# Attention with a two-pass gated layer behind it: the second pass's weights are decoded by other engines and at other points of the program

## The chip, the core and the metric

The kernel runs on one core of a Trainium2 chip. Its engines work side by side, each through its own list of instructions in order: PE (TensorE, matmuls, with its weight loads PEld), DVE (VectorE), ACT (ScalarE), POOL (GpSimd) and SP (SyncE), which here issues all DMAs. SBUF is the on-chip memory, PSUM holds the results of matmuls. The metric is the device time of one execution in microseconds.

## The reference

Eight batches of eight heads with 576 tokens of 64 features go through a linear attention with exponential features, and its output, as 4608 tokens of 512 features, through a gated layer of width 1536:

```python
def phi(x):
    proj = np.einsum('bhsd,df->bhsf', x, w_phi)
    proj = proj - np.max(np.abs(proj), axis=-1, keepdims=True)
    return np.concatenate([np.exp(proj), np.exp(-proj)], axis=-1)
q_p, k_p = (phi(q), phi(k))
kv = np.einsum('bhsf,bhsd->bhfd', k_p, v)
z = np.sum(k_p, axis=2)
num = np.einsum('bhsf,bhfd->bhsd', q_p, kv)
den = np.einsum('bhsf,bhf->bhs', q_p, z)[..., None] + 1e-06
x = (num / den).transpose(0, 2, 1, 3).reshape(4608, 512)
out = ((x @ w_a) * (x @ w_b)) @ w_out
```

The inputs `moe_w_a`, `moe_w_b` and `moe_w_out` reach the kernel in 64-bit floating point, as pairs of 32-bit words.

## The kernel before

**Precision.** Most matmuls are done on values split in two parts: `hi` is the value rounded to the matmul's format (fp32r), `lo` the rest, and a product is hi*hi + hi*lo + lo*hi. The helper `split` (L143 to L146) makes the parts: a cast on one engine (recorded as L139 on ACT), then a subtraction on another (recorded as L146).

**Stages.** The attention fills the first part. It writes unnormalised outputs to DRAM (`xun`) and the reciprocal denominators (`rec`). The gated layer runs in two passes over its width, slices of 128:

- *First pass*, six slices (`NFS[0]`), 16 blocks of 288 tokens, `moe_block(0, j)`. A block loads x (`load_x`: a DMA for x, DMAs for the reciprocals `rb`, the product L527, a split). Then for each slice f it makes `pa` and `pb` (12 matmuls each, L559), copies pa to SBUF on ACT (L563), multiplies on DVE (`h`, L564) and splits h into `hh` and `hl`. At the end, four outputs `po` of 18 matmuls each (L582), copied to `o` by ACT (L585) and written to the DRAM tensor `part`. So a block is 216 matmuls of 288 columns.
- *Second pass*, the other six slices, nine blocks of 512 tokens, `second_pass`. The slices are taken in three pairs q with Winograd's form of a 2x2 product (`winograd`, L642): it needs seven combinations of the weights for a and for b (`w11`, `w12`, `s1` to `s4`, `w22`) and the same of x (`factors_of_x`, L604 to L607). The results are gathered in `top` and `low` (L648 to L661), `h` is formed (L664 to L666) and split, and the outputs (`outputs`, L689) add `part` from DRAM (L694).

**The weights.** A raw load brings 128 x 512 pairs of words (`load_raw`, tile `raw`, two buffers). `decode` (L435 to L439) makes of them a rounded value s and a rest g with one ACT and four DVE instructions. `load_weights` makes `hi` and `lo` of a slice of w_out from them (L464 to L466). `load_factors` does it for a pair q and one of a and b: two decodes with a sum each (`w32`, L477), the sums s1 to s4 (L483 on DVE, L484 to L486 on POOL) and seven splits, with the cast on ACT and the subtraction on POOL. The places of the results (`places`) are 18 tiles of their own for the first pair and two `o` slices, and the places of the first pass's weights for the rest; those come free as the last block of the first pass uses them for the last time.

**Order.** The code is written as Python generators that yield between steps; the order in which they are drained is the program's order. The framework's scheduler then sets the order on each engine, with the program's order as its priority. While the attention runs, a queue `work` holds the blocks of the first pass whose x is ready, and they are drained at a pace between the attention's turns. Behind it, `ahead` (weights of pair 0 and two slices of w_out) and `more` (the remaining weights) are advanced a step at a time between the steps of the last blocks and of the second pass.

**PSUM.** The first pass's accumulators come from `ps_moe` with three buffers. `ps_late` with five buffers exists once the attention is over; a block takes the pool that was last appended to `pools_moe` when its first step runs (`psum = pools_moe[-1]`). Before the change that is `ps_moe` for blocks 0 to 13 and `ps_late` for 14 and 15.

Of the kernel before, what the change touches and what calls it, by code (L numbers as in the profile page):

```python
# [14 lines left out]
ALU = mybir.AluOpType  # L15
# [18 lines left out]
DECODE_TURN, X_LAG, BLOCK_LAG = 2, 2, 8  # L34
# [16 lines left out]

SLICES0 = 6
T2 = 512


@with_exitstack
def tile_kernel(ctx, tc, qT, km, kr, vm, vr, w_phi, w_a, w_b, w_out, out):
# [13 lines left out]
    nc = tc.nc  # L71
    B, H, _, S = qT.shape
# [7 lines left out]
    NCC = DM // P  # L80
    TS = (HALF, T2)
    NFS = (SLICES0, DF // P - SLICES0)
# [60 lines left out]
    def split(hi, lo, src, eng_hi, eng_lo):  # L143

        copy(eng_hi, hi, src)
        eng_lo.tensor_tensor(lo, src, hi, op=ALU.subtract)  # L146
# [274 lines left out]
    def decode(raw, u, stage):  # L421

        low, high = raw[:, :, 0], raw[:, :, 1]
        w = stage("w", [P, 2 * DM], F32, f"w_{u}")
        g, s = w[:, :DM], w[:, DM:]
        gb, sb = g.bitcast(U32), s.bitcast(U32)
        nc.scalar.mul(g, high.bitcast(F32), 2.0**-112)  # L435
        nc.vector.tensor_scalar(gb, gb, 3, None, op0=ALU.logical_shift_left)
        nc.vector.scalar_tensor_tensor(sb, high, 0x80000000, gb, op0=ALU.bitwise_and, op1=ALU.bitwise_or)
        nc.vector.tensor_scalar(gb, sb, 0xFF800000, None, op0=ALU.bitwise_and)
        nc.vector.scalar_tensor_tensor(g, low, 2.0**-52, g, op0=ALU.mult, op1=ALU.mult)  # L439
        return s, g  # L440

    def load_raw(p, f, nm, stage):

        cols = (sum(NFS[:p]) + f) * P
        src = {"a": w_a, "b": w_b, "o": w_out}[nm]
        raw = stage("raw", [P, DM, 2], U32, f"raw_{p}_{f}_{nm}")
        if nm == "o":
            nc.sync.dma_start(raw.rearrange("p n w -> p (n w)"), src[cols : cols + P, :].bitcast(U32))
        else:
            nc.sync.dma_start(  # L450
                raw.rearrange("p (c n) w -> p c (n w)", c=NCC),
                src.bitcast(U32)[:, 2 * cols : 2 * (cols + P)].rearrange("(c p) n -> p c n", p=P),
            )
        return raw

    def load_weights(p, f, names, stage, place=None):
        for nm in names:
            u = f"{p}_{f}_{nm}"
            s, g = decode(load_raw(p, f, nm, stage), u, stage)
            hi, lo = (  # L460
                pool.tile([P, DM], F32R, tag=tag, name=f"w{part}_{u}")
                for part, (pool, tag) in zip("hl", place or ((wpool, f"wh_{f}_{nm}"), (wpool, f"wl_{f}_{nm}")))
            )
            nc.scalar.copy(hi, s)  # L464
            nc.vector.tensor_tensor(s, s, hi, op=ALU.subtract)
            nc.vector.tensor_tensor(lo, s, g, op=ALU.add)  # L466
            weights[(p, f, nm)] = (hi, lo)
            yield

    def load_factors(q, nm, stage, places):  # L470

        w = []
        for i in range(2):
            u = f"q{q}_{nm}_{i}"
            s, g = decode(load_raw(1, 2 * q + i, nm, stage), u, stage)
            w.append(stage("w32", [P, DM], F32, f"w32_{u}"))
            nc.vector.tensor_tensor(w[i], s, g, op=ALU.add)  # L477
            yield
        n = DM // 2
        (w11, w12), (w21, w22) = ((t[:, :n], t[:, n:]) for t in w)  # L480
        sums = stage("ws", [P, 4, n], F32, f"ws_q{q}_{nm}")
        s1, s2, s3, s4 = (sums[:, i] for i in range(4))
        nc.vector.tensor_tensor(s1, w21, w22, op=ALU.add)  # L483
        nc.gpsimd.tensor_tensor(s3, w11, w21, op=ALU.subtract)  # L484
        nc.gpsimd.tensor_tensor(s2, s1, w11, op=ALU.subtract)
        nc.gpsimd.tensor_tensor(s4, w12, s2, op=ALU.subtract)  # L486
        factors = dict(w11=w11, w12=w12, s2=s2, s1=s1, s3=s3, w22=w22, s4=s4)
        yield
        for k, w32 in factors.items():
            pool, tag = places.popleft()  # L490
            t = pool.tile([P, 2, n], F32R, tag=tag, name=f"wf_q{q}_{nm}_{k}")
            split(t[:, 0], t[:, 1], w32, nc.scalar, nc.gpsimd)
            weights[(q, nm, k)] = t
            if k == "s1":
                yield
        yield

# [175 lines left out]
    def second_pass(xin):  # L673
        xs = yield from factors_of_x(0, xin)
        pool = xpools[1]
        for j in range(NT // T2):
# [38 lines left out]
            for cc in range(NCC):  # L715
                outputs(cc, range(0 if cc == NCC - 1 else early.stop, NFS[1]))
                yield

    def run(work, steps=None):

        while work and steps != 0:
            if next(work[0], work) is work:
                work.popleft()
            elif steps is not None:
                steps -= 1
# [3 lines left out]
    with ExitStack() as c:  # L729
        pools = attention_pools(c)  # L730
        consts = attention_consts(pools[0])
        work, tasks, due, st = deque(), {}, 0.0, {}
        tasks[DECODE_TURN] = []
        for names in ("ab", "o"):
            stage = stage_shared(pools[1])
            tasks[DECODE_TURN] += [load_weights(0, f, names, stage) for f in range(NFS[0])]
        for turn, ready in attention_steps(pools, consts, st):
            if ready is not None:
                at = turn + BLOCK_LAG
                tasks[at] = [moe_block(0, ready * per + h) for h in range(per)]  # L740
            for t in sorted(tasks):
                if t <= turn:
                    work.extend(tasks.pop(t))
            due += PACE0 if turn < PACE0_UNTIL else PACE
            run(work, int(due))
            due -= int(due)
        run(work)
    for t in sorted(tasks):
        work.extend(tasks[t])
    pools_moe.append(ctx.enter_context(tc.tile_pool(name="ps_late", bufs=5, space=PSUM)))  # L750


# [2 lines left out]
    ab = deque((wpool, f"w{part}_{f}_{nm}") for f in range(NFS[0]) for nm in "ab" for part in "hl")  # L755
# [7 lines left out]
    stage = stage_own(xin, 2, 2)  # L763
# [2 lines left out]
    )  # L766
    second = second_pass(xin)
    last = work.pop()
    while work:
        run(work, 1)  # L770
        next(ahead, None)
    next(last)
    for f in range(NFS[0]):
        next(last)
        next(ahead, None)
        if f < NCC // 2:
            next(second)
    for _ in ahead:
        pass
    more = itertools.chain(*(load_factors(1, nm, stage, ab) for nm in "ab"))  # L780
    for _ in range(NCC):
        next(more, None)
        next(last, None)
    run(deque([last]))
    xstack.close()
    xpools.append(ctx.enter_context(tc.tile_pool(name="pool", bufs=1)))
    ab.extend(o)
    more = itertools.chain(
        more,
        *(load_factors(2, nm, stage, ab) for nm in "ab"),  # L790
        *(load_weights(1, f, "o", stage, [o.pop(), o.pop()]) for f in range(2, NFS[1])),
    )
    for i, _ in enumerate(more):
        if i % 3 == 2:
            next(second)
    run(deque([second]))

# [32 lines left out]
```

## Time and profile before

| | us |
|---|---|
| median of three runs | 1281.06 |
| the three runs | 1281.87, 1281.06, 1276.15 |
| the profiled execution | 1278.22 |
| its span, first to last instruction | 1276.1 |
| block 11 begins on PE | 687.4 |
| block 15 begins on PE | 811.3 |
| second pass begins on PE | 843.2 |

In the lines of the profile, L is a line of the kernel, then come the engine, the operation and `out<-in`; a row of the timeline starts with its start and its duration in us, and ends with the idle time of the engine before it and who ended that. A table of stages gives the busy time and the count of instructions of each engine in a stretch of the span, then PE's granted clock (1.00 is full), the share of the DMA engines and GB/s.

### The profile page before, as it was taken

Reading aid. Unit: us, or ns where it says so; the run is one execution under the profiler, and the core shown is the slowest. Engines: PE = TensorE matmul, PEld = TensorE weight load, DVE = VectorE, ACT = ScalarE, POOL = GpSimd, SP = SyncE. Lnnn points to the kernel's source line nnn. Section 1 sums busy time; section 2 is a strip of 40 time slices with the busy share of each in tenths; the row PEclk is TensorE's granted clock in tenths of the full one; section 3 lists DMA queues with packets and bytes.
Section 4 is the critical chain, followed back from the end, with each engine's and each line's share of the span. In section 5 each row is a group of like instructions: output and inputs, shape, how many; then the busy total and the mean of one; then the engine's idle time right before and its main releaser. Section 6 shows DMA issues by size and latency. Waiting matters only on the chain.

```text
span 1276.1 us, 23003 instructions
## 1 busy us (share of the span) xinstructions
PE 1237.6 (97%) x8588; PEld 1136.0 (89%) x8588; DVE 935.3 (73%) x1622; ACT 734.4 (58%) x1577; POOL 214.5 (17%) x130
## 2 busy tenths in 40 slices
PE   8999999999999999999999899979999999999998
PEld 4566788999999999999999899979999999999997
DVE  7989568998999999988965873588656556556443
ACT  5667668889888988888873442444223223223221
POOL 2332222212122221312220500460000000000000
PEclk9999999999999999999999999989999999999999
DMA  7665443453534434444225451142422322331221
GB/s 185 177 196 151 116 122 88 112 141 78 145 96 133 115 104 125 110 113 121 71 57 152 145 162 57 46 129 88 127 82 74 116 91 66 108 93 57 66 67 50
DMA packets 126287, 138.24 MB, mean 108 GB/s; under 512 B 39712, under 2 KB 92448, under 8 KB 126176
## 3 DMA queue, kind: packets, MB, share of 16 engines
q1 hardware_dynamic: 126176, 136.78, 37.9%
q8 instruction: 67, 1.10, 0.4%
q14 instruction: 44, 0.36, 0.1%
HBM read 108.12 MB, written 28.61 MB: 107 GB/s over the span
## 4 chain that ended last, share of the span: by engine, by line
PE 74%; DVE 12%; DMA 6%; ACT 5%; issue 3%; SPq 1%; POOL 0%; DVEq 0%; ACTq 0%; POOLq 0%
PE pab L642 21%; PE po L689 11%; PE pa L559 8%; PE pb L559 8%; PE po L582 8%; PE kvps L289 7%; PE pn L367 6%; PE pq L343 3%; PE pk L231 1%; DMA x<-xun 1%; PE pk L222 1%; DMA den<-xn 1%; DVE qs L151 1%; DMA rb<-rec 1%; DMA r<-den 1%
## 5 line engine op out<-in xcount | busy, mean ns | idle before, releaser
L347 POOL PARTITION_ALL_REDUCE mb<-p x64 | 156.0, 2437 | 501.5 <-ACT p L344 479.1
L559 PE MATMUL pa<-xh,wh_a 128*128 128x288 f32 x384 | 115.9, 302 | 3.9 <-ACT o L585 1.5
L559 PE MATMUL pb<-xh,wh_b 128*128 128x288 f32 x384 | 114.9, 299 | 2.4 <-ACT h L563 2.4
L582 PE MATMUL po<-hh,wh_o 128*128 128x288 f32 x384 | 110.8, 299 | 5.4 <-DVE h L564 2.4
L139 ACT CAST hh<-h 128x288 fp32r<-128x288 f32 (+1 forms) x150 | 72.7, 503 | 73.0 <-DVE h L564 44.7
L559 PE MATMUL pb<-xh,wl_b 128*128 128x288 f32 x384 | 114.4, 298 | 0.0
L559 PE MATMUL pa<-xh,wl_a 128*128 128x288 f32 x384 | 114.4, 298 | 0.0
L582 PE MATMUL po<-hl,wh_o 128*128 128x288 f32 x384 | 112.7, 296 | 1.7 <-DVE hl L146 1.7
L559 PE MATMUL pa<-xl,wh_a 128*128 128x288 f32 x384 | 113.2, 295 | 0.0
L582 PE MATMUL po<-hh,wl_o 128*128 128x288 f32 x384 | 112.9, 297 | 0.0
L559 PE MATMUL pb<-xl,wh_b 128*128 128x288 f32 x384 | 112.7, 293 | 0.0
L146 DVE TENSOR_TENSOR hl<-h,hh 128x288 fp32r<-128x288 f32 (+1 forms) x150 | 85.6, 583 | 23.1 <-ACT hh L139 22.9
L527 DVE TENSOR_TENSOR x<-x,rb 128x288 f32<-128x288 f32 (+1 forms) x100 | 57.3, 576 | 38.3 <-DMA x<-xun 27.2
L689 PE MATMUL po<-hl,wh_o 128*128 128x512 f32 x216 | 84.5, 391 | 0.0
L689 PE MATMUL po<-hh,wl_o 128*128 128x512 f32 x216 | 84.3, 390 | 0.0
L559 PEld LDWEIGHTS pa<-xh,wh_a 128*128 128x128 f32 x384 | 72.2, 188 | 8.3 <-ACT o L585 2.0
L689 PE MATMUL po<-hh,wh_o 128*128 128x512 f32 x216 | 79.2, 392 | 0.0
L642 PE MATMUL pab<-xth,wf_q_a_s 128*128 128x256 f32 x324 | 72.8, 287 | 5.1 <-ACT top L648 5.1
L582 PEld LDWEIGHTS po<-hh,wh_o 128*128 128x128 f32 x384 | 71.0, 188 | 6.5 <-DVE h L564 3.0
L559 PEld LDWEIGHTS pb<-xh,wh_b 128*128 128x128 f32 x384 | 72.2, 188 | 4.5 <-ACT h L563 3.8
L582 PEld LDWEIGHTS po<-hl,wh_o 128*128 128x128 f32 x384 | 72.6, 189 | 3.2 <-DVE hl L146 2.6
L559 PEld LDWEIGHTS pa<-xl,wh_a 128*128 128x128 f32 x384 | 72.9, 190 | 0.6 <-issue 0.2
(226 smaller groups left out, 3858.8 us busy)
## 6 DMA issues: line engine op xcount, KB each, us to landing
q<-in_qT SPq DMA_DIRECT2D x110, 144.0 KB
k<-in_km SPq DMA_DIRECT2D x55, 256.0 KB
xun<-xn SPq DMA_DIRECT2D x64, 144.0 KB
x<-xun SPq DMA_DIRECT2D x64, 144.0 KB
rb<-rec SPq DMA_DIRECT2D x128, 72.0 KB
part<-o SPq DMA_DIRECT2D x16, 576.0 KB
o<-part SPq DMA_DIRECT2D x36, 256.0 KB
out_x<-o SPq DMA_DIRECT2D x36, 256.0 KB
```

Source lines behind the costliest of these rows:

```text
L139: eng.copy(dst, src)
L146: eng_lo.tensor_tensor(lo, src, hi, op=ALU.subtract)
L151: eng_lo.tensor_tensor(hi_lo[D:], src[D:], hi_lo[D:], op=ALU.subtract)
L289: nc.tensor.matmul(st["kv_ps", b, pr][:width, j], v_[:, j, :width], e_[:, j], start=(left == NFULL and j == 0 and n_ == 0), stop=(left == ...
L343: nc.tensor.matmul(pq[:, :HALF], w_, q_[:, tok], start=(n_ == 0), stop=(n_ == len(parts) - 1))
L347: nc.gpsimd.partition_all_reduce(mb, p32, P, bass_isa.ReduceOp.absmax)
L367: nc.tensor.matmul(pn[: D + 1, :HALF], kv_[:, 2 * j + s, :], e_[:, s, tok], **at)
L527: nc.vector.tensor_tensor(x32, x32, rb, op=ALU.mult)
L559: nc.tensor.matmul(acc, w[:, cc * P : (cc + 1) * P], x, start=(k == 0), stop=(k == 3 * NCC - 1))
L582: nc.tensor.matmul(acc, w[:, cc * P : (cc + 1) * P], h, start=(k == 0), stop=(k == 3 * NFS[p] - 1))
L642: nc.tensor.matmul(acc[to][:, i], w_, x_, skip_group_check=True, **at)
L689: nc.tensor.matmul(acc[cc], w[:, cc * P : (cc + 1) * P], h, **at)
```

## The change

1. `decode` yields twice, `load_weights` once more per tile, and `load_factors` after other splits: the steps are smaller. The first pass's own weights are wrapped in `whole`, which takes all steps of a tile at once.
2. The sums s2 to s4 and the subtractions of the splits in `load_factors` go from GpSimd to VectorE. POOL is left with the attention's reductions.
3. The attention part of the program leaves five blocks (`BLOCKS_LAST`) in the queue instead of draining it; `ps_late` is created and `ahead` begins there. `ahead` is advanced by 0.7 steps per step of a block (`AHEAD`).
4. The first two x factors of the second pass stand ahead of the last block; `more` is advanced two steps per step of the last block.
5. In the second pass's first block its steps are taken after every ninth step of `more`.

```diff
+BLOCKS_LAST, AHEAD = 5, 0.7
@@ decode
         nc.vector.tensor_scalar(gb, gb, 3, None, op0=ALU.logical_shift_left)
+        yield
         nc.vector.scalar_tensor_tensor(sb, high, 0x80000000, gb, op0=ALU.bitwise_and, op1=ALU.bitwise_or)
         nc.vector.tensor_scalar(gb, sb, 0xFF800000, None, op0=ALU.bitwise_and)
+        yield
         nc.vector.scalar_tensor_tensor(g, low, 2.0**-52, g, op0=ALU.mult, op1=ALU.mult)
@@ load_weights
-            s, g = decode(load_raw(p, f, nm, stage), u, stage)
+            s, g = yield from decode(load_raw(p, f, nm, stage), u, stage)
...
             nc.vector.tensor_tensor(s, s, hi, op=ALU.subtract)
+            yield
             nc.vector.tensor_tensor(lo, s, g, op=ALU.add)
@@ load_factors
-            s, g = decode(load_raw(1, 2 * q + i, nm, stage), u, stage)
+            s, g = yield from decode(load_raw(1, 2 * q + i, nm, stage), u, stage)
...
         nc.vector.tensor_tensor(s1, w21, w22, op=ALU.add)
-        nc.gpsimd.tensor_tensor(s3, w11, w21, op=ALU.subtract)
-        nc.gpsimd.tensor_tensor(s2, s1, w11, op=ALU.subtract)
-        nc.gpsimd.tensor_tensor(s4, w12, s2, op=ALU.subtract)
+        nc.vector.tensor_tensor(s3, w11, w21, op=ALU.subtract)
+        nc.vector.tensor_tensor(s2, s1, w11, op=ALU.subtract)
+        nc.vector.tensor_tensor(s4, w12, s2, op=ALU.subtract)
...
-            split(t[:, 0], t[:, 1], w32, nc.scalar, nc.gpsimd)
+            split(t[:, 0], t[:, 1], w32, nc.scalar, nc.vector)
             weights[(q, nm, k)] = t
-            if k == "s1":
+            if k in ("w12", "s1", "w22"):
                 yield
@@ the program
-            tasks[DECODE_TURN] += [load_weights(0, f, names, stage) for f in range(NFS[0])]
+            tasks[DECODE_TURN] += [whole(load_weights(0, f, nm, stage)) for f in range(NFS[0]) for nm in names]
...
-        run(work)
-    for t in sorted(tasks):
-        work.extend(tasks[t])
+        for t in sorted(tasks):
+            work.extend(tasks[t])
+        while len(work) > BLOCKS_LAST:
+            run(work, 1)
     pools_moe.append(ctx.enter_context(tc.tile_pool(name="ps_late", bufs=5, space=PSUM)))
...
+    due = 0.0
     while work:
         run(work, 1)
-        next(ahead, None)
+        due += AHEAD
+        while due >= 1:
+            next(ahead, None)
+            due -= 1
+    for _ in ahead:
+        pass
+    for _ in range(NCC // 2):
+        next(second)
     next(last)
     for f in range(NFS[0]):
         next(last)
-        next(ahead, None)
-        if f < NCC // 2:
-            next(second)
-    for _ in ahead:
-        pass
-    more = itertools.chain(*(load_factors(1, nm, stage, ab) for nm in "ab"))
-    for _ in range(NCC):
-        next(more, None)
-        next(last, None)
-    run(deque([last]))
+    ab.extend(o)
+    more = itertools.chain(
+        *(load_factors(q, nm, stage, ab) for q in range(1, NFS[1] // 2) for nm in "ab"),
+        *(load_weights(1, f, "o", stage, [o.pop(), o.pop()]) for f in range(2, NFS[1])),
+    )
+    for _ in last:
+        next(more)
+        next(more)
     xstack.close()
...
     for i, _ in enumerate(more):
-        if i % 3 == 2:
+        if i % 9 == 5:
             next(second)
```

With the change, blocks 12 to 15 take their accumulators from `ps_late`; block 11's first step still runs while `ps_moe` is the last pool. The instructions of every engine stand in the same order in both programs up to the start of block 11. In block 13 and block 14 no step of a decode stands on DVE in either. The lines of the changed kernel are shifted: L439, L441, L442 and L444 are the four DVE instructions of `decode`, L483 the sum behind it, L438 its ACT instruction, L570 the product `h`, L142 and L149 the cast and the subtraction of a split.

DVE at the start of block 11, before (`h32_0_11_f` is h of block 11 and slice f, `w_q0_a_i` the work tile of a decode, `x32_0_12_1` the x of block 12):

```order
L379 RECIPROCAL r_7_3_8767<-r_7_3_8767 128x9
L527 TENSOR_TENSOR x32_0_12_1_9824<-x32_0_12_1_9824,rb_0_12_1_9825 128x288
L564 TENSOR_TENSOR h32_0_11_0_9560<-pb_0_11_0_9547,h32_0_11_0_9560 128x288
L436 TENSOR_SCALAR w_q0_a_0_10508<-w_q0_a_0_10508 128x512
L437 SCALAR_TENSOR_TENSOR w_q0_a_0_10508<-raw_1_0_a_10506,w_q0_a_0_10508 128x512
L146 TENSOR_TENSOR hl_0_11_0_9564<-h32_0_11_0_9560,hh_0_11_0_9563 128x288
```

The same place on DVE with the change:

```order
L382 RECIPROCAL r_7_3_8767<-r_7_3_8767 128x9
L439 TENSOR_SCALAR w_q0_a_0_9614<-w_q0_a_0_9614 128x512
L441 SCALAR_TENSOR_TENSOR w_q0_a_0_9614<-raw_1_0_a_9612,w_q0_a_0_9614 128x512
L533 TENSOR_TENSOR x32_0_12_1_9856<-x32_0_12_1_9856,rb_0_12_1_9857 128x288
L442 TENSOR_SCALAR w_q0_a_0_9614<-w_q0_a_0_9614 128x512
L439 TENSOR_SCALAR w_q0_a_1_9756<-w_q0_a_1_9756 128x512
L444 SCALAR_TENSOR_TENSOR w_q0_a_0_9614<-raw_1_0_a_9612,w_q0_a_0_9614 128x512
L441 SCALAR_TENSOR_TENSOR w_q0_a_1_9756<-raw_1_1_a_9754,w_q0_a_1_9756 128x512
L483 TENSOR_TENSOR w32_q0_a_0_9719<-w_q0_a_0_9614 128x512
L442 TENSOR_SCALAR w_q0_a_1_9756<-w_q0_a_1_9756 128x512
L570 TENSOR_TENSOR h32_0_11_0_9572<-pb_0_11_0_9559,h32_0_11_0_9572 128x288
```

Eight instructions of two decodes have moved ahead of the product of slice 0. On SP, the two raw loads they read (`raw_1_0_a`, `raw_1_1_a`) have moved ahead of six rb loads and stand right behind the load of `r_7_3`.

ACT at the start of the second pass, before (`top_1_0_q` belongs to pair q of the second pass's first block, `wf_q2_b_*` are splits of pair 2, `w_1_f_o` is the decode of slice f of w_out, `o_0_15` the output of block 15):

```order
L139 CAST wf_q2_b_w22_11637<-w32_q2_b_1_11589 128x256
L435 ACTIVATE w_1_2_o_11645<-raw_1_2_o_11643 128x512
L139 CAST wf_q2_b_s1_11605<-ws_q2_b_11591 128x256
L585 COPY o_0_15_11218<-po_0_15_3_11306 128x288
L139 CAST wf_q2_b_s3_11634<-ws_q2_b_11591 128x256
L139 CAST wf_q2_b_s2_11602<-ws_q2_b_11591 128x256
L464 CAST wh_1_2_o_11651<-w_1_2_o_11645 128x512
L139 CAST wf_q2_b_s4_11640<-ws_q2_b_11591 128x256
L435 ACTIVATE w_1_3_o_11658<-raw_1_3_o_11656 128x512
L648 COPY top_1_0_0_11363<-pab0_1_0_0_11360 128x512
```

And with the change:

```order
L591 COPY o_0_15_11208<-po_0_15_3_11289 128x288
L142 CAST wf_q2_b_w11_11527<-w32_q2_b_0_11510 128x256
L142 CAST wf_q2_b_w12_11530<-w32_q2_b_0_11510 128x256
L142 CAST wf_q2_b_w22_11611<-w32_q2_b_1_11520 128x256
L438 ACTIVATE w_1_2_o_11619<-raw_1_2_o_11617 128x512
L654 COPY top_1_0_0_11353<-pab0_1_0_0_11350 128x512
L142 CAST wf_q2_b_s1_11605<-ws_q2_b_11522 128x256
```

The first copy of `top` has moved ahead of the four casts of the sums, of the cast of slice 2 of w_out and of the decode of slice 3; three more casts of pair 2 now stand between the block's last output and it.

More of the change, by code (lines that the diff above doesn't have):

```diff
@@ L717, in second_pass, with whole @@
                 yield
+    def whole(steps):
+        for _ in steps:
+            pass
+        yield
     def run(work, steps=None):
@@ L768, in tile_kernel @@
     last = work.pop()
+    due = 0.0
     while work:
         run(work, 1)
-        next(ahead, None)
+        due += AHEAD
[3 more added lines that the diff above has]
+    for _ in ahead:
+        pass
+    for _ in range(NCC // 2):
+        next(second)
     next(last)
@@ L774, in tile_kernel @@
         next(last)
-        next(ahead, None)
-        if f < NCC // 2:
-            next(second)
-    for _ in ahead:
-        pass
-    more = itertools.chain(*(load_factors(1, nm, stage, ab) for nm in "ab"))
-    for _ in range(NCC):
-        next(more, None)
-        next(last, None)
-    run(deque([last]))
+    ab.extend(o)
[6 more added lines that the diff above has]
+        next(more)
     xstack.close()
     xpools.append(ctx.enter_context(tc.tile_pool(name="pool", bufs=1)))
[L787 to L792, printed above, removed]
     for i, _ in enumerate(more):
-        if i % 3 == 2:
+        if i % 9 == 5:
             next(second)
```

## The prediction

> **What bounds the kernel now.** I read the page first, then the table of stages, then the timelines of single engines where a stage falls short.
>
> ```profile
> span 1276.1 us, 23003 instructions
> PE 1237.6 (97%) x8588; PEld 1136.0 (89%) x8588; DVE 935.3 (73%) x1622; ACT 734.4 (58%) x1577; POOL 214.5 (17%) x130
> L347 POOL PARTITION_ALL_REDUCE mb<-p x64 | 156.0, 2437 | 501.5 <-ACT p L344 479.1
> ```
>
> PE (TensorE) is busy for 97% of the span, so nothing is won except where PE stands still. POOL (GpSimd) spends 214.5 - 156.0 = 58.5 us outside the reductions of the attention, in 130 - 64 - 6 = 60 instructions (six set up constants): the sums and splits of the second pass's weights.
>
> ```profile
> 700.00:750.00 50.00, 42.83 (x307) 40.75 (x307) 45.31 (x86) 23.88 (x58) 17.12 (x18) 1.00 0.49 145
> 750.00:800.00 50.00, 50.00 (x380) 50.00 (x379) 20.16 (x43) 14.94 (x36) 2.42 (x3) 1.00 0.30 89
> 830.00:840.00 10.00, 7.46 (x52) 6.78 (x52) 9.60 (x15) 4.20 (x12) 7.88 (x10) 1.00 0.31 103
> 840.00:850.00 10.00, 10.00 (x83) 10.00 (x82) 8.23 (x10) 4.86 (x13) 8.04 (x10) 1.00 0.31 107
> 850.00:860.00 10.00, 4.95 (x25) 4.75 (x24) 8.39 (x13) 4.45 (x9) 4.98 (x5) 0.70 0.64 191
> 860.00:870.00 10.00, 10.00 (x83) 10.00 (x82) 9.20 (x19) 4.72 (x9) 0.00 (x0) 0.96 0.54 162
> 1050.00:1100.00 50.00, 50.00 (x354) 47.05 (x353) 28.02 (x52) 14.80 (x29) 0.00 (x0) 1.00 0.32 95
> ```
>
> The columns are the stretch, its length, then PE, PEld, DVE, ACT, POOL (busy us and count), the granted clock, the DMA share and GB/s. The undisturbed stretch 750:800 issues 380 matmuls of 288 columns, 0.1316 us each. In 700:750 there are 73 fewer: **9.6 us lost** (blocks 11 and 12 of the first pass). 830:840 has 52 where 76 fit: **3.2 us** (end of block 15). The matmuls of 256 columns go at 84 in 10 us (0.119 us); 850:870 has 108 of 168: **7.1 us** (start of the second pass). Together 19.9 us. From 900 on PE is full (1050:1100), and neither its work nor its waits change there.
>
> Why PE stood, from its timeline (start, duration, and in brackets the idle time and who ended it):
>
> ```profile
> 708.81 0.40 PE L582 MATMUL po<-hh,wh_o 128*128 128x288 f32 x1 [1.70 <-DVE h L564]
> 718.15 0.40 PE L582 MATMUL po<-hh,wh_o 128*128 128x288 f32 x1 [1.65 <-ACT o L585]
> 725.47 0.40 PE L559 MATMUL pa<-xh,wh_a 128*128 128x288 f32 x1 [1.50 <-ACT o L585]
> 741.32 0.40 PE L559 MATMUL pa<-xh,wh_a 128*128 128x288 f32 x1 [1.10 <-ACT h L563]
> 833.35 0.40 PE L582 MATMUL po<-hh,wh_o 128*128 128x288 f32 x1 [1.25 <-ACT hh L139]
> 855.61 0.58 PE L642 MATMUL pab<-xth,wf_q_a_s 128*128 128x256 f32 x1 [5.05 <-ACT top L648]
> ```
>
> ACT is named often, but it was itself queued behind DVE or POOL. Ahead of the copy of `top` (L648) stand:
>
> ```profile
> 852.75 0.40 ACT L139 CAST wf_q_b_s<-ws_q_b 128x256 fp32r<-128x256 f32 x1 [1.97 <-POOL ws_q_b L486]
> 854.42 0.66 ACT L435 ACTIVATE w_o<-raw_o 128x512 f32<-128x512 f32 x1 [1.27 <-DVE wl_o L466]
> ```
>
> So the limit in these places is DVE with POOL. And DVE is slow there:
>
> ```profile
> 703.09 0.45 DVE L564 TENSOR_TENSOR h<-pb,h 128x288 f32<-128x288 f32 x1
> 704.24 1.00 DVE L146 TENSOR_TENSOR hl<-h,hh 128x288 fp32r<-128x288 f32 x1
> 705.15 0.96 DVE L438 TENSOR_SCALAR w_q_b<-w_q_b 128x512 uint32<-128x512 uint32 x1
> 706.15 1.11 DVE L439 SCALAR_TENSOR_TENSOR w_q_b<-raw_b,w_q_b 128x512 f32<-128x512 uint32 x1
> ...
> 728.09 0.68 DVE L439 SCALAR_TENSOR_TENSOR w_o<-raw_o,w_o 128x512 f32<-128x512 uint32 x1
> 728.69 0.68 DVE L465 TENSOR_TENSOR w_o<-w_o,wh_o 128x512 f32<-128x512 f32 x1
> 729.29 0.45 DVE L146 TENSOR_TENSOR hl<-h,hh 128x288 fp32r<-128x288 f32 x1
> 729.66 0.68 DVE L466 TENSOR_TENSOR wl_o<-w_o 128x512 fp32r<-128x512 f32 x1
> ...
> 733.57 0.42 DVE L605 TENSOR_TENSOR xs<-x,xs 128x256 f32<-128x256 f32 x1
> 734.91 0.42 DVE L604 TENSOR_TENSOR xs<-x 128x256 f32<-128x256 f32 x1
> ```
> ```profile
> 705.79 0.91 POOL L486 TENSOR_TENSOR ws_q_a<-w_q_a,ws_q_a 128x256 f32<-128x256 f32 x1
> 706.67 2.31 POOL L146 TENSOR_TENSOR wf_q_a_s<-ws_q_a,wf_q_a_s 128x256 fp32r<-128x256 f32 x2
> ```
>
> Beside a running POOL a subtraction of 128x288 takes 1.00 us instead of 0.45, L439 1.11 instead of 0.68. With POOL silent, starts follow each other by 0.60 us (128x512: 728.09 to 729.29 in two steps), 0.37 (128x288) and 0.335 (128x256: between 733.57 and 734.91 lie four steps). Only L564, which reads PSUM, keeps its 0.45. The Trainium skill (GPSIMD Engine Reference, 8. Key points) says that GpSimd shares its SBUF interfaces with VectorE and contends with instructions that have two SBUF inputs or run in a 2-port mode; the rows agree, L564 included, and by that rule the slowness goes with POOL and not with the DMA traffic of that time.
>
> **The change, part by part.** (1) *60 instructions go from POOL to DVE.* All have the 128x256 shape: 60 x 0.335 = 20.1 us more on DVE, instead of 58.5 us on POOL. In return DVE regains its normal pace. In block 15, from the first product `h` to the last:
>
> ```profile
> 814.76 0.46 DVE L564 TENSOR_TENSOR h<-pb,h 128x288 f32<-128x288 f32 x1 [8.88 <-PE pb L559]
> 835.48 0.45 DVE L564 TENSOR_TENSOR h<-pb,h 128x288 f32<-128x288 f32 x1
> ```
>
> That took 20.7 us for 8 short, 10 middle and 10 long instructions, at normal pace 8 x 0.335 + 10 x 0.37 + 10 x 0.60 = 12.4. The new order has 21 short, 10 middle and 7 long ones there: 7.0 + 3.7 + 4.2 = 14.9 us. PE needs 5 x 24 x 0.1316 = 15.8 us for the same slices. DVE now just keeps up; before it was 5 us behind. The 3.2 us go; I leave 0.5 for places where a split waits for its cast.
>
> (2) *The start of the second pass.* From the last `h` of block 15 to the decode that frees ACT for the first copy of `top`, the new order has 18 short, 1 middle and 8 long DVE instructions: 6.0 + 0.4 + 4.8 = 11.2 us, and about 1 us in which casts wait behind ACT's copy of the block's last output; then 0.67 for L435 and 0.6 for the copy, 13.5 us in all. PE needs this copy 72 x 0.1316 + 60 x 0.119 = 16.6 us after the last pb. Margin 3 us: the 5.05 us wait goes, and with it the half clock (0.70 in 850:860), 7.1 us in all; I leave 0.5. What is late next: DVE has the last splits and four `o` weights still ahead of it. Up to the splits of `h` that PE needs for its first outputs stand 22 short and 24 long instructions, 7.4 + 14.4 = 21.8 us. In the new order 228 of the 256-column matmuls stand before them on PE, 228 x 0.119 = 27.1 us into the pass. DVE starts the 21.8 at 11.2 + 1 + 0.4 - 72 x 0.1316 = 3.1 us into it and waits 1 to 2 us for x factors, whose loads now stand behind two loads of `part` in SP's queue: done at 26 to 27. Before, 0.4 us lay between them (DVE's pair ends at 876.96, PE's first use is at 877.39). I leave 2.0 us.
>
> ```profile
> 875.67 1.29 DVE L146 TENSOR_TENSOR hl<-h,hh 128x512 fp32r<-128x512 f32 x2
> 877.39 0.40 PE L689 MATMUL po<-hl,wh_o 128*128 128x512 f32 x1
> ```
>
> (3) *Decode ahead of block 11's own work.* The order puts eight decode instructions before `h` of slice 0 on DVE, and two L435 before ACT's copies of block 10's last output and of the first pa. They wait for raw weights; those loads move up past six rb loads on SP.
>
> ```profile
> 682.63 0.32 SPq L377 DMA_DIRECT2D r<-den  x1
> 688.05 0.52 SPq L450 DMA_DIRECT2D raw_a<-in_w_a  x1
> ```
> ```profile
> 687.39 0.29 PE L559 MATMUL pa<-xh,wh_a 128*128 128x288 f32 x1
> 692.48 0.66 ACT L435 ACTIVATE w_q_a<-raw_a 128x512 f32<-128x512 f32 x1 [2.84 <-DMA raw_a<-in_w_a]
> ```
>
> They leave right behind r<-den, at 683.0 instead of 688.05. The first took 4.4 us then (688.05 to 692.48), so 687.4; the second follows by 688 to 689.6. The second L435 takes 0.67, and the six DVE instructions from there to the end of `h`, 2 x 0.335 + 3 x 0.60 + 0.37 = 2.8 us, so `h` is there at 691.5 to 693.1. PE needs it when the third pa starts, 687.39 + 2 x 24 x 0.1316 = 693.7. It holds, barely, and slices 1 to 3 run with DVE full: I leave 1.0 us. Behind an `h` that is late stand on DVE its own split and the next decode, and PE waits for both. The six rb loads that are passed go 1.0 us later (two issues of 0.52); they are for block 12, and block 11's 216 x 0.1316 = 28.4 us of matmuls cover that.
>
> (4) *Block 12 and 13 get five PSUM buffers instead of three*, since the later pool now exists when they begin: `h` may be two slices late instead of one. With the pace of (1) block 12 has some 3 us of margin; I leave 0.5 for x factors that DVE waits for in its order. (5) *Single steps.* The order shows no decode row between block 13 and block 14 in either program: the splits need places that block 15 frees. And the sums and splits of the first x factors (L604 to L607) stand in block 12's part of the order in both. So I count these two edits at zero: no row of block 13 or 14 changes its place on PE or DVE. Were the steps really spread there, DVE (20.16 of 50 us busy in 750:800) would hide 20 us of them.
>
> Sum: 19.9 - (0.5 + 0.5 + 2.0 + 1.0 + 0.5) = **15.4 us gained**. The profiled execution took 1278.2 us (span 1276.1 and 2.1 around it), so 1262.8. The three runs have 1276.15, 1281.06 and 1281.87; with the profiled one their mean is 1279.6, so I put the forecast 1.4 higher, at **1264**.
>
> Bounds of the unknown: what stays of the waits is between nothing (1259.7 on this scale) and, in the start of the second pass, everything (7.1 more than the best).
>
> **Rivals.** *All waits go*, 1279.6 - 19.9 = 1260. For: the margins above are all positive. Against: four of them are under 1.5 us.
>
> *DVE becomes the bound.* A DVE instruction that needs the one before it starts later than the 0.335 of independent ones; if each of the some 60 instructions of (1) and (2) lost 0.1 us, `top` would come 6 - 3 = 3 us late and the splits another 2. A 3 us wait would also bring back part of the half clock (24 matmuls took 855.61 to 860.88, 2.4 us over 24 x 0.119). 1264 - 1 + 3 + 2 + 2 = 1270. The Trainium skill (TensorE: Matmul & The Clock Gate, Part 1) has TensorE fall to half rate after an idle window of about 3.4 us; the waits of 1.70 us with clock 1.00 and the one of 5.05 with 0.70 agree.
>
> *The loads set the pace*, not DVE: raw weights have two buffers, and each load waits until a decode frees one. Four pairs after block 15's first slices, each 4.4 for the load and about 3 for ACT and DVE, make 29.6 us, against 28.4 + 7.1 of PE. If loads take 6 us or more in pairs, the waits only change names: 1278 to 1280.
>
> *Slower:* the slowness came from something else than POOL (DMA was at 317 GB/s nearby), and the 60 instructions cost on DVE what POOL's cost, 0.975 us. Block by block DVE would then be over PE's time. The gain is used up at (20.1 + 19.9) / 60 = 0.67 us each; at 0.975 PE would lose 60 x 0.31 = 18 us: 1298. Against it: 850:870 with DMA at 0.5 and more, where POOL is silent after 860 and DVE is at full pace.
>
> **How the numbers follow.** Forecast 0.53, all waits gone 0.12, DVE the bound 0.19, loads set the pace 0.10, slower 0.06. The range takes the first three in: 1257 to 1274. Half a percent (6.4 us) is about what a measurement can tell from no change: 0.53 + 0.12 and most of 0.19 lie beyond it: faster 0.82, same 0.12, slower 0.06.
>
> **What would show it.** Right: 307 in 700:750 becomes about 370, POOL zero after the attention, L146 of 128x288 at 0.45 throughout, no wait of `pab` over 1 us and clock 1.00 in the first 20 us of the second pass. Wrong: DVE at 0.9 us or more without POOL (then the fourth rival), PE waiting in slice 2 of block 11 for `h` behind a raw load, or a wait at the first `top` or at the first outputs for `hl`.

## The result, and the profile after

| | before | after |
|---|---|---|
| median, us | 1279.53 (1276.15 to 1281.87) | 1261.98 (1261.01 to 1263.61) |
| profiled execution: span | 1276.1 | 1260.6 |

The ratio is 0.9872, 95% interval 0.9854 to 0.9890: 1.3% faster, and the time lies 2 us under the forecast of 1264, in its range. All of it comes after the attention. From the start of block 11 to the end the span was 1276.1 - 687.39 = 588.7 us, and is 1260.6 - 689.72 = 570.9: 17.8 us less. (In the profiled execution after, block 11 began 2.3 us later; what is ahead of it stands in the same order in both programs, so the spans differ by 15.5 only.) Where block 11 and the second pass begin, from PE's timeline:

```profile
689.72 0.29 PE L565 MATMUL pa<-xh,wh_a 128*128 128x288 f32 x1
...
834.12 0.28 PE L648 MATMUL pab<-xfh,wf_q_a_w 128*128 128x256 f32 x1
```

The page of the changed kernel, busy time by engine:

```profile
PE 1229.8 (98%) x8588; PEld 1131.8 (90%) x8588; DVE 928.8 (74%) x1682; ACT 734.3 (58%) x1577; POOL 157.3 (12%) x70
```

POOL has lost its 60 instructions and 57 us. DVE has 60 more, and is busy for *less* time than before (935.3). The stages, in the columns of the table shown before:

```profile
700.00:750.00 50.00, 48.96 (x370) 48.73 (x369) 47.24 (x112) 26.65 (x64) 0.00 (x0) 1.00 0.55 168
830.00:840.00 10.00, 10.00 (x83) 10.00 (x82) 9.37 (x22) 5.44 (x14) 0.00 (x0) 1.00 0.52 177
840.00:850.00 10.00, 10.00 (x86) 10.00 (x85) 8.78 (x20) 5.29 (x12) 0.00 (x0) 1.00 0.60 180
850.00:860.00 10.00, 9.16 (x76) 8.96 (x76) 8.02 (x17) 3.96 (x9) 0.00 (x0) 1.00 0.37 115
```

700:750 has 370 matmuls instead of 307. The second pass runs at clock 1.00 from its first matmul on. Two waits of PE are left, from its timeline:

```profile
702.25 0.40 PE L565 MATMUL pb<-xh,wh_b 128*128 128x288 f32 x1 [1.04 <-ACT h L569]
855.27 0.39 PE L648 MATMUL pab<-xrh,wf_q_a_s 128*128 128x256 f32 x1 [0.84 <-DVE low L663]
```

The first stands in block 11: pb of slice 3 needs the PSUM buffer from which ACT copies pa of slice 2, and that copy (L569) stood behind a decode that waited for its raw load, and behind two casts, as ACT's timeline shows:

```profile
700.65 0.66 ACT L438 ACTIVATE w_q_b<-raw_b 128x512 f32<-128x512 f32 x1 [1.44 <-DMA raw_b<-in_w_b]
701.22 0.70 ACT L142 CAST wf_q_a_s<-ws_q_a 128x256 fp32r<-128x256 f32 x2
701.82 0.38 ACT L569 COPY h<-pa 128x288 f32<-128x288 f32 x1
```

The second is of the same kind, on DVE: a product of x (L533) waits for rb, and the addition of `low` stands behind it, with three instructions between them.

```profile
844.70 0.69 DVE L533 TENSOR_TENSOR x<-x,rb 128x512 f32<-128x512 f32 x1 [1.22 <-DMA rb<-rec]
...
852.38 0.69 DVE L533 TENSOR_TENSOR x<-x,rb 128x512 f32<-128x512 f32 x1 [1.98 <-DMA rb<-rec]
852.99 0.42 DVE L439 TENSOR_SCALAR w_o<-w_o 128x512 uint32<-128x512 uint32 x1
853.33 0.69 DVE L444 SCALAR_TENSOR_TENSOR w_o<-raw_o,w_o 128x512 f32<-128x512 uint32 x1
853.93 0.69 DVE L470 TENSOR_TENSOR w_o<-w_o,wh_o 128x512 f32<-128x512 f32 x1
854.53 0.68 DVE L663 TENSOR_TENSOR low<-pab,low 128x512 f32<-128x512 f32 x1
```

### The profile page after: what moved, and what is told of

Read it like the earlier page. It is cut to its first block, busy times and chain, and to the rows that moved or that the text cites. A ratio compares the mean times of both kernels' runs of the same rounds, so it can differ in the third digit from the quotient of the medians.

```text
span 1260.6 us, 22965 instructions
## 1 busy us (share of the span) xinstructions
PE 1229.8 (98%) x8588; PEld 1131.8 (90%) x8588; DVE 928.8 (74%) x1682; ACT 734.3 (58%) x1577; POOL 157.3 (12%) x70
## 4 chain that ended last, share of the span: by engine, by line
PE 76%; DVE 9%; DMA 6%; ACT 5%; issue 2%; SPq 1%; POOL 0%; DVEq 0%; ACTq 0%
PE pab L648 21%; PE po L695 11%; PE pa L565 10%; PE pb L565 10%; PE po L588 9%; PE kvps L292 6%; PE pn L370 5%; PE pq L346 2%; DMA raw_b<-in_w_b 1%; PE pk L234 1%; DVE qs L154 1%; DMA rb<-rec 1%; DMA r<-den 1%; DVE kd L240 1%; DVE kel L149 1%
## 5 line engine op out<-in xcount | busy, mean ns | idle before, releaser
L142 ACT CAST hh<-h 128x288 fp32r<-128x288 f32 (+1 forms) x150 | 72.7, 503 | 70.7 <-DVE h L570 40.7
L149 DVE TENSOR_TENSOR hl<-h,hh 128x288 fp32r<-128x288 f32 (+1 forms) x150 | 81.2, 554 | 22.7 <-ACT hh L142 22.5
L533 DVE TENSOR_TENSOR x<-x,rb 128x288 f32<-128x288 f32 (+1 forms) x100 | 56.0, 564 | 37.8 <-DMA x<-xun 26.2
L565 PEld LDWEIGHTS pa<-xh,wl_a 128*128 128x128 f32 x384 | 72.1, 188 | 1.3 <-issue 1.1
L565 PEld LDWEIGHTS pb<-xl,wh_b 128*128 128x128 f32 x384 | 72.8, 190 | 0.3
```

Source lines behind the costliest of these rows:

```text
L142: eng.copy(dst, src)
L533: nc.vector.tensor_tensor(x32, x32, rb, op=ALU.mult)
L565: nc.tensor.matmul(acc, w[:, cc * P : (cc + 1) * P], x, start=(k == 0), stop=(k == 3 * NCC - 1))
```

## The experiments

The theory to be tested (A): GpSimd slows VectorE by running beside it, and the move removed that. Its rivals: (B) the earlier start of the decode and the five PSUM buffers bring the gain; (C) VectorE and ScalarE had waited for GpSimd's *results*, and the slower instructions beside it mattered little; (D) VectorE has slack, so that only a part of GpSimd's work hurts. "Before" was run again beside each group of kernels, with medians of 1280.0, 1280.5 and 1278.8. Kernels of different groups are best compared by their ratios to it; where that gives another number than the medians, both stand.

| run | median, us | ratio to before, 95% |
|---|---|---|
| after | 1261.98 | 0.9854 to 0.9890 |
| after, the 60 back on GpSimd | 1274.93 | 0.9947 to 0.9981 |
| before, only the 60 moved | 1262.48 | 0.9831 to 0.9917 |
| before, two edits of the change | 1261.71 | 0.9823 to 0.9884 |
| after, 60 unused more on GpSimd | 1283.07 | 1.0006 to 1.0041 |
| after, 18 sums on GpSimd | 1262.50 | 0.9820 to 0.9888 |
| after, 42 splits on GpSimd | 1273.05 | 0.9926 to 0.9960 |
| after, 60 unused more on VectorE | 1267.81 | 0.9876 to 0.9939 |
| after, four steps left | 1262.06 | 0.9834 to 0.9885 |
| after, the 60 left out | 1262.28 | 0.9849 to 0.9912 |
| the same, 60 unused on GpSimd | 1273.04 | 0.9928 to 0.9971 |
| after, rb on ACT's queue | 1262.58 | 0.9852 to 0.9898 |

**The parts alone.** First the changed kernel with the 60 instructions back on GpSimd:

```diff
-        nc.vector.tensor_tensor(s3, w11, w21, op=ALU.subtract)
+        nc.gpsimd.tensor_tensor(s3, w11, w21, op=ALU.subtract)
...
-            split(t[:, 0], t[:, 1], w32, nc.scalar, nc.vector)
+            split(t[:, 0], t[:, 1], w32, nc.scalar, nc.gpsimd)
```

> The changed kernel with the 60 sums and splits back on GpSimd; all the rest stays (decode in block 11, five PSUM buffers in blocks 12 and 13, single steps, x factors). Theory A, the move off GpSimd brings most of the gain, since DVE runs at its normal pace only with POOL silent: 1270 to 1278 us, L149 of 128x288 again near 1.0 us beside POOL, a wait of several us at the first copy of top. Rival B, the earlier start and the buffers bring it: 1261 to 1265, whatever DVE's pace.

It took 1274.93 us, 12.9 more than after (11.8 by the ratios). Of the change's 17.5 us some 4.6 are left. The scheduler also sets another order on PE, VectorE and ScalarE here, so the run shows the move together with that order. The wait at the first copy of `top` is back, and with it the half clock, a granted clock of 0.66 from 850 to 860: behind the wait the matmuls take 0.58 and 0.41 us, where behind the wait of 0.84 us above the first one took 0.39.

```profile
853.08 0.58 PE L648 MATMUL pab<-xth,wf_q_a_s 128*128 128x256 f32 x1 [5.04 <-ACT top L654]
853.46 0.41 PE L648 MATMUL pab<-xtl,wf_q_a_s 128*128 128x256 f32 x1
```
```profile
850.00:860.00 10.00, 6.92 (x40) 6.92 (x41) 8.68 (x15) 4.92 (x9) 2.45 (x3) 0.66 0.64 179
```

Then the kernel before with the opposite edit and nothing else:

> The kernel before with only the move of the 60 instructions from GpSimd to VectorE; raw loads, PSUM buffers and order rules stay as they were. Theory A: 1262 to 1267 us, the 7.1 us of the second pass's start and the 3.2 us of block 15 gone, L146 of 128x288 at 0.45 us throughout; some of the 9.6 us of blocks 11 and 12 may stay, since the decode still starts 5 us later. Rival B: 1274 to 1280.

1262.48 us: the move alone brings all that can be measured (with it, here too, the order that the scheduler then sets). The other edits together bring 4.6 us while GpSimd works in these stretches, and none that shows once it does not. The two gains don't add.

Third, the kernel before with the move and this:

```diff
-        run(work)
-    for t in sorted(tasks):
-        work.extend(tasks[t])
+        for t in sorted(tasks):
+            work.extend(tasks[t])
+        while len(work) > BLOCKS_LAST:
+            run(work, 1)
     pools_moe.append(ctx.enter_context(tc.tile_pool(name="ps_late", bufs=5, space=PSUM)))
```

> The kernel before with two edits of the change alone: the move to VectorE, and the later PSUM pool opened when five steps of work are left. No single steps, no x factors moved, no pacing. If those others count zero, as the prediction had them: the time of the changed kernel, 1260.5 to 1264 us. If they carry some of the gain: 1265 or more.

1261.71 us. In this program PE's instructions stand in the same order as in the changed kernel; on DVE and on ACT one instruction stands a place or two away, on SP one load. So, once the 60 are on VectorE, the single steps, the x factors ahead of the last block and the new pacing move next to nothing: the scheduler gives the same order from the coarser steps.

**Contention without waiting.** The helper `dose` issues subtractions that nothing waits for, after each split of the changed kernel:

```diff
+    def dose(t, times):
+        for _ in range(times):
+            nc.gpsimd.tensor_tensor(spill[0], t[:, 0].bitcast(F32), t[:, 1], op=ALU.subtract)
...
             split(t[:, 0], t[:, 1], w32, nc.scalar, nc.vector)
+            dose(t, 2 if k in ("w12", "s1", "w22") else 1)
```

> The changed kernel with 60 more GpSimd subtractions of 128x256 that nothing waits for: each reads a finished pair of split halves and writes a scratch tile. The output stays the same. Theory A (POOL slows DVE by running beside it): L149 of 128x288 near 1.0 us while POOL runs, some 57 us of DVE at 0.6 of its pace, which is over 20 us of DVE time, and 1270 to 1285 us. Rival C (before lost its time by waiting for POOL's results, not by contention): 1261 to 1264, L149 at 0.45.

1283.07 us: 21 us (19.5 by the ratios) lost to work that nobody needs, while the order on the other engines is that of the changed kernel. (C) can't explain that. But VectorE has 60 instructions more here than before the change. So a second pair of kernels leaves the 60 out, and differs in nothing but GpSimd's list:

```diff
-        nc.vector.tensor_tensor(s3, w11, w21, op=ALU.subtract)
-        nc.vector.tensor_tensor(s2, s1, w11, op=ALU.subtract)
-        nc.vector.tensor_tensor(s4, w12, s2, op=ALU.subtract)
-        factors = dict(w11=w11, w12=w12, s2=s2, s1=s1, s3=s3, w22=w22, s4=s4)
+        factors = dict(w11=w11, w12=w12, s2=s1, s1=s1, s3=s1, w22=w22, s4=s1)
...
-            split(t[:, 0], t[:, 1], w32, nc.scalar, nc.vector)
+            nc.scalar.copy(t[:, 0], w32)
...
-    for n_, (w_, x_) in enumerate(((w[:, 0, cols], xh), (w[:, 0, cols], xl), (w[:, 1, cols], xh))):
+    for n_, (w_, x_) in enumerate(((w[:, 0, cols], xh), (w[:, 0, cols], xl), (w[:, 0, cols], xh))):
```

In the second kernel of the pair `dose` stands behind the cast and reads the high half twice.

> The changed kernel with the 60 sums and splits left out: the products that use a low half or a sum take the high half or s1 in its place, so PE, ACT and the loads do the same work, and nothing runs on GpSimd after the attention. The output is not the reference's. It shows what those 60 instructions still cost on VectorE: all theories say 1259 to 1262.5 us, since only some 2 us of waits were left.

> The kernel that leaves the 60 out, in the same order on PE, VectorE, ScalarE and SyncE, with 60 GpSimd subtractions of 128x256 beside it that nothing waits for (each reads a finished high half and writes scratch). VectorE has then the work that it had before the change, with the contention but without a wait for a GpSimd result. Theory A, contention is what the move removed: 1270 to 1276 us, near the 1274.9 of the run with the real ones back on GpSimd. Rival C, the waits for GpSimd's results are what it removed: 1260 to 1264.

1262.28 and 1273.04 us. VectorE's timelines of the two can be laid side by side, since each has the same instructions in the same order. Block 15 from the first `h` on, the 60 left out, nothing on GpSimd:

```profile
807.28 0.46 DVE L570 TENSOR_TENSOR h<-pb,h 128x288 f32<-128x288 f32 x1
808.46 0.43 DVE L439 TENSOR_SCALAR w_q_b<-w_q_b 128x512 uint32<-128x512 uint32 x1 [0.72 <-ACT w_q_b L438]
808.80 0.45 DVE L149 TENSOR_TENSOR hl<-h,hh 128x288 fp32r<-128x288 f32 x1
809.17 0.68 DVE L441 SCALAR_TENSOR_TENSOR w_q_b<-raw_b,w_q_b 128x512 uint32<-128x512 uint32 x1
809.89 0.43 DVE L442 TENSOR_SCALAR w_q_b<-w_q_b 128x512 uint32<-128x512 uint32 x1
...
823.26 0.45 DVE L570 TENSOR_TENSOR h<-pb,h 128x288 f32<-128x288 f32 x1
```

And with 60 unused subtractions on GpSimd:

```profile
808.76 0.46 DVE L570 TENSOR_TENSOR h<-pb,h 128x288 f32<-128x288 f32 x1
809.94 0.43 DVE L439 TENSOR_SCALAR w_q_b<-w_q_b 128x512 uint32<-128x512 uint32 x1 [0.72 <-ACT w_q_b L438]
810.28 0.87 DVE L149 TENSOR_TENSOR hl<-h,hh 128x288 fp32r<-128x288 f32 x1
811.07 1.10 DVE L441 SCALAR_TENSOR_TENSOR w_q_b<-raw_b,w_q_b 128x512 uint32<-128x512 uint32 x1
812.20 0.72 DVE L442 TENSOR_SCALAR w_q_b<-w_q_b 128x512 uint32<-128x512 uint32 x1
...
828.61 0.45 DVE L570 TENSOR_TENSOR h<-pb,h 128x288 f32<-128x288 f32 x1
```

From the first of the six products to the last it is 16.0 us without GpSimd, which is near PE's own pace (15.8), and 19.9 us with it. With the real ones back on GpSimd it is 20.7, against 15.6 in the changed kernel. So contention alone makes 3.9 us in this block where the real ones made 5.1. Of the whole time it makes 10.8 us (8.7 by the ratios), where the real ones made 12.9 (11.8). From the start of block 11 to the end, the two traces of the pair differ by 9.4 us (it starts at 687.01 and 686.80), and the trace with the real ones and that of the changed kernel by 13.3 (689.23 and 689.72). What is left for waits on GpSimd's results is 2 to 4 us. That is inside the intervals, and it holds two other things: GpSimd was busy for 10 us more with the real ones, and the order was another. So contention is the larger part, and (C) is not excluded for a small one. The wait of 5 us at the first copy of `top` is a place where it may count: with the unused ones it is 1.32 us.

The pages of the two give the price on VectorE:

```profile
PE 1232.0 (98%) x8588; PEld 1133.5 (90%) x8588; DVE 910.8 (72%) x1622; ACT 732.4 (58%) x1577; POOL 155.9 (12%) x70
```
```profile
PE 1235.6 (97%) x8588; PEld 1135.1 (89%) x8588; DVE 926.3 (73%) x1622; ACT 732.5 (58%) x1577; POOL 205.4 (16%) x130
```

and the same line with the 60 real ones back on GpSimd:

```profile
PE 1236.7 (97%) x8588; PEld 1135.5 (89%) x8588; DVE 935.7 (73%) x1622; ACT 733.9 (58%) x1577; POOL 215.3 (17%) x130
```

Without the 60, DVE is busy for 910.8 us. Doing them itself costs it 928.8 - 910.8 = 18.0 us. Having GpSimd do them costs it 935.7 - 910.8 = 24.9 us. The helper took more of VectorE's time than the work that it took over. The unused ones, which kept GpSimd busy for less time, cost it 926.3 - 910.8 = 15.5 us.

**How much of it, and how much room.** Only the three sums of each pair on GpSimd, then only the splits (the first and the second half of the first diff above):

> The changed kernel with only the 18 sums (three for each pair of weights) back on GpSimd; the 42 splits stay on VectorE. With all 60 back it lost 12.9 us. Theory A, the loss goes with the time that POOL runs beside DVE: 18 of 60, 12.9 x 0.3 = 3.9, so about 1266 us. Rival D, VectorE has slack for the first part of it and only the last instructions hurt: 1262 to 1263.

> The changed kernel with only the 42 splits back on GpSimd, the sums on VectorE. Theory A: 12.9 x 0.7 = 9.0, about 1271 us. Rival D: nearly all of the 12.9, 1273 to 1275.

1262.50 and 1273.05 us. By the medians 18 instructions cost 0.5 us, which can't be told from nothing, and 42 cost 11.1. This speaks for (D) and against my line of proportion: VectorE has slack, which the 17 us of the sums on GpSimd (POOL busy for 173.9 instead of 157.3 us) don't use up. But it is not shown. By the ratios the 42 cost 9.1 us, where proportion gives 9.0. The traced execution with the 18 sums, the slowest of its four at 1267.80 us, took 4.3 us more than the changed kernel's trace from the start of block 11 (690.85 there) to the end, where proportion gives 3.9, and has two waits for `low`:

```profile
853.19 0.38 PE L648 MATMUL pab<-xth,wf_q_a_w 128*128 128x256 f32 x1 [1.51 <-ACT low L662]
857.86 0.39 PE L648 MATMUL pab<-xth,wf_q_a_w 128*128 128x256 f32 x1 [1.54 <-ACT low L662]
```

Next, the 60 unused subtractions on VectorE itself:

```diff
-            nc.gpsimd.tensor_tensor(spill[0], t[:, 0].bitcast(F32), t[:, 1], op=ALU.subtract)
+            nc.vector.tensor_tensor(spill[0], t[:, 0].bitcast(F32), t[:, 1], op=ALU.subtract)
```

> The changed kernel with 60 more VectorE subtractions of 128x256 that nothing waits for, at the places where the earlier experiment had them on GpSimd (which cost 21 us there). Output unchanged. The prediction's break-even: VectorE has nothing left in these stretches and each moved instruction may cost 0.67 us before the gain is used up, so 60 x 0.335 = 20 us more of VectorE cost about as much: 1278 to 1282. Rival: VectorE still has slack for most of them, 1264 to 1270.

1267.81 us: 5.8 us for 20 us of work, where GpSimd's 60 had cost 21. The 1278 to 1282 expected from the prediction's break-even were wrong. There are two reservations. As nothing waits for them, the scheduler could put these 60 where they hurt little, and it changed the order of the others. And part of their bill came later, as PE's timeline shows, in an execution that was the slowest of its four at 1272.32 us:

```profile
879.21 0.50 PE L695 MATMUL po<-hh,wl_o 128*128 128x512 f32 x1 [2.36 <-DVE wl_o L472]
```

**The two waits that were left.** One kernel begins the decode a block later (`BLOCKS_LAST` 4 instead of 5), to take it out of block 11:

> The changed kernel with the later pool opened when four steps of work are left instead of five. If the wait of about 1 us in block 11 comes from the decode put there (a copy of pa behind a decode that waits for its raw load), it goes; block 12's part of the decode then comes later. Theory: no decode row in block 11's first slices, that wait gone, total within 1.5 us of the changed kernel, 1260.5 to 1263.5. Rival, the early start is worth something: 1265 or more.

1262.06 us. The wait in block 11 is gone. In its place block 12, now again with three PSUM buffers, has two, which come to as much:

```profile
734.05 0.40 PE L565 MATMUL pa<-xh,wh_a 128*128 128x288 f32 x1 [0.46 <-DVE h L570]
738.27 0.40 PE L565 MATMUL pa<-xh,wh_a 128*128 128x288 f32 x1 [0.78 <-DVE h L570]
```

The wait for `low` does not show in this trace, though DVE waits 0.97 and 1.09 us for rb at these places.

The other kernel issues the second pass's first rb loads from ACT:

```diff
-                nc.sync.dma_start(rb[i * D : (i + 1) * D, dst], rec[b][h : h + 1, src].broadcast_to([D, n]))
+                (nc.scalar if p == 1 and j == 0 else nc.sync).dma_start(rb[i * D : (i + 1) * D, dst], rec[b][h : h + 1, src].broadcast_to([D, n]))
```

> The changed kernel with the 32 loads of rb for the second pass's first x factors issued on ScalarE's queue instead of SyncE's. If the wait of 0.84 us for `low` (L663) comes from VectorE standing 2 us at an x product that waits for rb, behind loads of o weights and part on SyncE: that wait goes and the time is 0.5 to 1 us lower, 1260 to 1262. If ScalarE pays for the issues: same or up to 2 us higher.

1262.58 us, and the wait is still there. But the run does not test it. The edit moved eight loads, not 32: those of the x factors of the second pass's first block, whose products run from 716.65 to 726.46 and which ACT now issues from 712.5 to 722.2. The x that DVE waits for belongs to the pass's second block, and its rb loads are still issued by SP, behind two loads of `part`, as in the changed kernel:

```profile
712.52 1.13 ACTq L531 DMA_DIRECT2D rb<-rec  x2
```
```profile
838.67 0.81 SPq L699 DMA_DIRECT2D o<-part  x2
839.53 5.91 SPq L531 DMA_DIRECT2D rb<-rec  x9
```
```profile
844.28 0.69 DVE L533 TENSOR_TENSOR x<-x,rb 128x512 f32<-128x512 f32 x1 [0.99 <-DMA rb<-rec]
...
852.06 0.69 DVE L533 TENSOR_TENSOR x<-x,rb 128x512 f32<-128x512 f32 x1 [1.80 <-DMA rb<-rec]
```
```profile
854.94 0.39 PE L648 MATMUL pab<-xrh,wf_q_a_s 128*128 128x256 f32 x1 [1.06 <-DVE low L663]
```

So it stays open whether SyncE's queue makes rb late. There are also only two rb buffers, and the load that DVE waits for can't start before an earlier product has freed one. In this trace SP's next load of rb leaves at 845.00, just as the product of 844.28 ends (844.97). That may be the cause, and a third buffer was not tried. No version was faster than the changed kernel by more than can be measured.

## Why the prediction was right, point by point

*The base.* The mean of the four executions before is 1279.3 us, not 1279.6. This makes the forecast 1263.9 and changes nothing.

*The bound.* 19.9 us of lost PE time were counted. All but 1.9 went (1.04 and 0.84), which makes 18.0; measured from block 11 on it is 17.8, and 17.5 by the medians.

*The residues.* 4.5 us were left, 1.9 stayed:

| | left | measured |
|---|---|---|
| block 15 | 0.5 | 0 |
| first copy of `top` | 0.5 | 0 |
| `hl` of the first outputs | 2.0 | 0, but 0.84 at `low` |
| block 11 | 1.0 | 1.04 |
| blocks 12 and 13 | 0.5 | 0 |

In block 11 the size came out, and the mechanism in part. `h` of slice 0 was put at 4.1 to 5.7 us behind the block's first matmul. It was done 6.4 us behind it, at 696.13, and PE began the third `pa` at 696.19. So what was to hold barely did hold, by less than 0.1 us. The 1.04 us came one slice later and on another engine: a raw load was late, as a sign against the forecast had it, but it held up ACT's copy of pa and not the product on DVE.

```profile
695.68 0.45 DVE L570 TENSOR_TENSOR h<-pb,h 128x288 f32<-128x288 f32 x1
```

At the second pass's start the cause was named, DVE waiting for x factors, but not its victim, and it was larger: 1.22 and 1.98 us, 3.2 together, instead of 1 to 2. Their loads do stand behind two loads of `part` on SP, as the prediction had it; whether that is why they are late was not tested. `hl` was done when PE came to it, by 0.02 us:

```profile
861.94 1.29 DVE L149 TENSOR_TENSOR hl<-h,hh 128x512 fp32r<-128x512 f32 x2
```
```profile
863.25 0.40 PE L695 MATMUL po<-hl,wh_o 128*128 128x512 f32 x1
```

This zero is in part luck. DVE was done 29.1 us into the pass, not at 26 to 27. PE came at 29.1 instead of 27.1, held up mainly by the 0.84 us at `low` and by three matmuls of 512 columns with `hh` that the sum had left out.

The margin of 3 us at `top` was really 1.7: ACT's copy ends at 839.55, and PE comes to its next product at 834.12 + 60 x 0.119 = 841.26.

```profile
838.96 0.59 ACT L654 COPY top<-pab 128x512 f32<-128x512 f32 x1 [0.44 <-DMA part<-o]
```

*The mechanism.* L149 of 128x288 takes 0.45 us from block 11 on in the changed kernel, and near 0.9 again beside a running GpSimd, whether anyone waits for GpSimd or not. That is the rule that the prediction took from the rows, and the pair without the 60 shows it with everything else held fixed. DVE in block 15 was put at 14.9 us against PE's 15.8; from the first `h` to the last it took 15.6, of which it stood idle for 0.5:

```profile
809.32 0.45 DVE L570 TENSOR_TENSOR h<-pb,h 128x288 f32<-128x288 f32 x1
...
824.90 0.45 DVE L570 TENSOR_TENSOR h<-pb,h 128x288 f32<-128x288 f32 x1
```

*The steps counted at zero.* They were, with the 60 on VectorE: the kernel with two edits has the same time. A decode's last steps do run on DVE in the first 4 us of block 13, before and with the change, but ahead of its first product.

*The rivals.* The fourth one, slow instructions that stay on DVE, had no ground. But the break-even that I gave for it, 0.67 us per moved instruction, was mis-sized. It set each us on DVE equal to one on PE. The 60 cost nothing measurable at 0.30 us each (1261.98 with them, 1262.28 without), and at twice that only 5.8 us of the 17.5 were gone. *The loads set the pace* was seen at one place for the raw weights, for 1.04 us. *DVE becomes the bound* did not happen: `top` had 1.7 us to spare.

*What I did not see.* The two large parts of the change, each alone, were not priced. Had they been, the table above would have shown that the move suffices, and that the other edits help only as long as VectorE is slow.

## What to carry to other kernels

Before a second engine is given elementwise work, look at what the first one's own instructions take while it runs: here 24.9 us of VectorE's time went to save 18.0. Test contention with work that nobody waits for, in a pair of programs that differ in nothing else; a wait for the helper's results and the slowness that it spreads look alike in a chain of waits. When a load is moved to test a wait, make sure from the trace that it is the load that is waited for. And when several edits come together, run the largest alone: one accounted for all of it, and, with that one in place, three changed hardly a row of the order that the scheduler made.

## What the runs showed of the hardware

Beside a GpSimd subtraction of 128x256, VectorE's instructions with two inputs in SBUF took longer: L149 of 128x288 0.87 us instead of 0.45, L441 of 128x512 1.10 instead of 0.68. L442, with one input, went from 0.43 to 0.72; L439, also with one, kept 0.43 at 809.94 and took 0.77 at 816.50. L570, which reads one input from PSUM, kept 0.46. GpSimd's subtractions took 0.75 to 0.85 us on average meanwhile. Its list, grouped, in the kernel with the 60 left out and 60 unused on GpSimd:

```profile
L63 POOL TENSOR_TENSOR spill<-wf_q_b_w 128x256 fp32r<-128x256 f32 x15 | 12.7, 849 | 4.6 <-ACT wf_q_b_w L498 3.4
L63 POOL TENSOR_TENSOR spill<-wf_q_a_s 128x256 fp32r<-128x256 f32 x15 | 11.3, 750 | 3.1 <-ACT wf_q_a_s L498 2.1
```

The Trainium skill (SBUF — State Buffer, Who interferes with whom) says that a VectorE instruction with two SBUF inputs contends with a GpSimd instruction that reads SBUF, and that the ports they share are an exclusive lock. L149, L441 and L570 agree with the first. The rows do not show the lock itself: L149 took about as long as GpSimd's instructions, L441 longer.

The half clock of PE came behind waits of 5.05 and 5.04 us, and the wait of 1.70 us in block 11 before left the clock at 1.00. But one long wait is not needed for it. With the 60 left out and 60 unused on GpSimd it came in block 15, behind waits of 0.92 and 0.57 us that lie close together:

```profile
827.09 0.40 PE L588 MATMUL po<-hh,wh_o 128*128 128x288 f32 x1 [0.92 <-ACT hh L142]
828.06 0.40 PE L588 MATMUL po<-hl,wh_o 128*128 128x288 f32 x1 [0.57 <-DVE hl L149]
```
```profile
828.50:832.00 3.50, 3.50 (x17) 3.50 (x16) 3.46 (x6) 2.12 (x6) 2.84 (x4) 0.51 0.17 60
```

And with 60 unused on VectorE it came behind the wait of 2.36 us, with a granted clock of 0.53 from 879.5 to 883. So the rule that the prediction quoted beside its second rival fits the two waits that it named, and not these.
